# Attention, two expert layers and a gate in one kernel: the counts as a running sum, two groups' attention sums with the queries in the rows, and a longer planned wait for GpSimd

## The chip, the core and the metric

One core of a Trainium2 chip runs the whole program. The metric is device microseconds of one execution; lower is better. The engines are named as the profile names them: PE is TensorE (PEld its weight loads), DVE is VectorE, ACT is ScalarE, POOL is GpSimd, SP is the queue that issues most DMAs.

## What is computed

```
# q, k, v: (2, 8, 768, 64); n_sink = 4; window = 128
keep = (key < n_sink) | ((query - key >= 0) & (query - key < window))
s = where(keep, q @ k.T / sqrt(64), -1e9)
a = exp(s - max(s)); a = a / (sum(a) + 1e-9)
x = (a @ v), heads side by side                 # 1536 tokens x 512
h = x @ w_in; x = max(0.01 * h, h) @ w_out      # 512 -> 2048 -> 512
do = (x @ w_skip) > 0                           # skip gate
e = argmax(x @ w_gate); gate = softmax(x @ w_gate)[e]   # 8 experts
out = x; out[do] += gate * (relu(x @ w1[e]) @ w2[e])    # 512 -> 1024 -> 512
```

All of it is float32.

## The kernel before

The 1536 tokens are six groups g = 0 to 5 of 256 tokens (two tiles of 128 each, twelve tiles t in all). Three stages overlap: attention of a group, the dense layer of a group (sixteen chunks f of 128 hidden columns: `chunk`, L868 for the first product, L889 for the second), and the gate of a group (`gating`). The eight experts come last (`plan_routed`, L1109, L1119, L1126).

**Order.** No engine's order is written by hand. `Plan.op` collects every operation with its engine, a cost in ns, what it reads and writes and a priority; `Plan.run` simulates five queues with these costs, gives each engine the ready operation of lowest priority number for which a buffer is free, and emits instructions in that order. `Plan.gap(a, b)` is the wait that the plan allows between the end of a and the start of a dependent b: 195 ns from PE, 150 ns between other engines. At run time each engine works through its own list strictly in turn. Whether an instruction waits there is decided on the chip, not by the plan.

**Attention of groups 0 and 1** ("whole" in the code) keeps plain float32 matmuls. `blocks` loads q, k and v of the group into buffers of the tag `w`. For v it takes, for every 128 keys, a buffer of 4 x 2 x 128 columns in which each head's 64 columns stand beside 64 columns that POOL has set to zero (L373), so that two heads can add into one 128-row result. For each pair of heads p = 0 to 3, `prep` turns keys and queries (L458, L468; copies on ACT and DVE at L462, L478, L475). For each half qt of the queries, `item` makes for both heads h the scores (PE, L591), adds the mask and takes the row's minimum (DVE, L598), takes the exponential and its sum (ACT, L601), adds 1e-9 and inverts the sums (DVE, L605, L606), scales the weights P by the inverse (L610 on ACT, L613 on POOL), turns P (PE, L629) into a copy AT (ACT, L633), and multiplies (PE, L668) with v as the stationary and AT as the moving operand; keys of the sink block come in by a further matmul per head with `vs` stationary and `wz` (buffer C) moving, for all items but those of group 0. The result PV has the 128 columns of the two heads in its rows and the 128 queries in its columns, which is what the dense layer reads: ACT copies it to x (L674) and DVE makes the low part (L675). The float32 matmuls appear as two records each in the trace.

Group 0 scales head 0 on POOL and head 1 on ACT, group 1 both on ACT, groups 2 to 5 both on POOL.

**Counts.** `gating` needs, for every token of tile t, how many earlier tokens chose the same expert. The one-hot choices of all tiles stand in `oh_all` (128 x 8 for a tile, bfloat16). Tile t takes t matmuls of `ones` against the earlier tiles' one-hots and one of `tri` against its own (L1015), accumulated in PSUM. `count_over` adds up all twelve (L1046). For the last group the two tiles are gated one after the other, and the `ones` part is emitted apart from the `tri` part. There the count is followed by L1024 (DVE, the selection columns `hs`) and L844 (PE, which gathers the first expert's tokens by it). L974 is a small matmul that folds the gate's two half products (`fold`, 18 rows by 9 columns moving).

Of the kernel before, what the change touches and what calls it, by code (L numbers as in the profile page):

```python
# [47 lines left out]
C_TR = 114.0  # L48
C_DMA = 490.0
# [17 lines left out]
class Plan:  # L67
# [166 lines left out]
class Arm:  # L234
# [63 lines left out]
    def keep(self):  # L298

        k = lambda name, shape, dt=F32: self.pool.tile(shape, dt, tag=name, bufs=1, name=name)  # L300
        self.oh_all = k("oh_all", [128, self.NT // 128, self.E], BF16)
        self.rank_all = k("rank_all", [128, self.NT // 128])
        self.gate_all = k("gate_all", [128, self.NT // 128])
        self.nt = k("nt", [128, 2, self.E])
        self.tot = k("tot", [128, 2], I32)
        self.w9 = k("w9", [128, 4, 2, 9], F32R)
        self.ks = k("ks", [128, self.KD, 16])

    def share(self, other):
        for name in ("pool", "psum", "oh_all", "rank_all", "gate_all", "nt", "tot", "w9"):  # L310
            setattr(self, name, getattr(other, name))


# [24 lines left out]
    def blocks(self, g, b, qp):  # L338

        P, nc, io = self.p, self.nc, self.io  # L340
        if qp == 0:
            self.raws = {}
        pr = -60 if g == 0 else -13.5
        def ld(t, a, p0, p1):

            heads, n = slice(2 * p0, 2 * p1), p1 - p0
            src = io[t][b, heads, 128 * a:128 * a + 128, :]
            if t != "v":
                eng, dma = ("ACT", nc.scalar) if g == 0 and t == "k" and p0 == 0 else ("SP", nc.sync)
                x = self.raws[t, a // 2]  # L350
                P.op(eng, C_DMA, lambda: dma.dma_start(
                    out=x.tile[:, a % 2, 128 * p0:128 * p1].rearrange("p (h d) -> p h d", d=64), in_=src.rearrange("h p d -> p h d")),
                    w=[(x, (a % 2, p)) for p in range(p0, p1)], pr=pr, lat=64 * n * 1024 / 200.0)
                return
            x = self.raws[t, a]
            for h in range(2):
                P.op("SP", C_DMA, lambda h=h: nc.sync.dma_start(
                    out=x.tile[:, p0:p1, h, 64 * h:64 * h + 64], in_=io["v"][b, 2 * p0 + h:2 * p1:2, 128 * a:128 * a + 128, :].rearrange("h p d -> p h d")),
                    w=[(x, (h, 0))], pr=pr, lat=32 * n * 1024 / 200.0)

        new = range(2 * qp, 2 * qp + 2)
        for t in "qk":
            self.raws[t, qp] = P.buf("w", [128, 2, 512])
        for p0, p1 in ((0, 1), (1, self.KD)) if g == 0 else ((0, self.KD),):
            for t in "kq":
                for a in new:
                    ld(t, a, p0, p1)
            if p0 == 0:
                for a in new:

                    x = self.raws["v", a] = P.buf("w", [128, self.KD, 2, 128])
                    for h in range(2):
                        P.op("POOL", 100 + 0.9 * 256, lambda x=x, h=h: nc.gpsimd.memset(x.tile[:, :, h, 64 - 64 * h:128 - 64 * h], 0.0), w=[(x, (h, 1))], pr=pr)  # L373
                    if g:
                        ld("v", a, 0, self.KD)
        if g == 0:
            for a in new:
                ld("v", a, 0, self.KD)

    def load(self, g, b, qp, p):  # L380

# [18 lines left out]
    def sinks_v(self, g, b, whole):  # L400
        P, nc, io = self.p, self.nc, self.io
        pr = 16 * (g - 1) - 7
        src = lambda h: io["v"][b, h:self.H:2, 0:16, :].rearrange("h s d -> s h d")
        vs = self.vs = P.buf("vs", [128, self.KD, 2, 128], F32 if whole else F32R)
        if whole:
            def ld():
                for h in range(2):
                    nc.sync.dma_start(out=vs.tile[h:32:2, :, h, 64 * h:64 * h + 64], in_=src(h))
# [4 lines left out]
            P.op("POOL", 1000, lambda: nc.gpsimd.memset(vs.tile, 0.0), w=[vs], pr=pr - 7)  # L413
# [152 lines left out]
    def item(self, g, qp, p, qt, whole):  # L566

        P, nc, c = self.p, self.nc, self.c
        pr = self.order(g, p, qt)
        qb = 2 * qp + qt  # L570
        one, sink = qb == 0, qb >= 2
        ncol = 128 if one else 272
# [11 lines left out]
        sm = P.buf("s4", [128, 2])  # L584
# [19 lines left out]

        P.op("DVE", 70, lambda: nc.vector.tensor_scalar(out=sm.tile, in0=sm.tile, scalar1=1e-9, scalar2=None, op0=ALU.add), w=[sm], pr=pr)  # L605
        P.op("DVE", 81, lambda: nc.vector.reciprocal(out=sm.tile, in_=sm.tile), w=[sm], pr=pr)  # L606
        for h in range(2):
            if g == 1 or g == 0 and h:

                P.op("ACT", c_act(ncol, False), lambda h=h: nc.scalar.activation(out=A.tile[:, 0:ncol, h], in_=A.tile[:, 0:ncol, h], func=AF.Copy, scale=sm.tile[:, h:h + 1]),  # L610
                     r=[sm], w=[(A, h)], pr=pr)
# [25 lines left out]
                out=x.tile[:, :, 1, :], in0=tt.tile[:, 2 * i:2 * i + 2, :], in1=x.tile[:, :, 0, :].bitcast(F32), op=ALU.subtract), r=[tt, (x, 0)], w=[(x, 1)], pr=pr)  # L637
        js = [1] if one else [qt, qt + 1]
        if whole:
            vb = [self.raws["v", 2 * qp - 1 + j] for j in js]  # L640
            rd = [*AT, *vb]
            vblk = lambda i, h: vb[i].tile[:, p, h, :]
        else:
            rd = [*AT, vh]
            vblk = lambda i, h: vh.tile[:, js[i], h, :]
# [12 lines left out]
        vs = self.vs  # L658
        pv = P.buf(spare if g == 2 else "PV", [128, 2, 256])

        def pvmm():
            for h in range(2):
                mm = [(vblk(i, h), at(i, h)) for i in range(len(js))]
                if sink:
                    mm.append((vs.tile[:, p, h, :], wz.tile if whole else self.sAT.rearrange("p a b -> p (a b)")))
                for n, (l, r) in enumerate(mm):
                    to = pv.tile[:, 0, 0:128] if whole else pv.tile[:, h, :]
                    nc.tensor.matmul(out=to, lhsT=l, rhs=r, start=n == 0 and not (whole and h), stop=n == len(mm) - 1 and (h == 1 or not whole))  # L668

        P.op("PE", (nj + 2 * sink) * (213 if whole else c_mm(256)), pvmm, r=rd, w=[pv], pr=pr)  # L670
        if whole:
            xT = self.xt[g]
            x = lambda i: xT.tile[:, i, p, 128 * qt:128 * qt + 128]
            P.op("ACT", c_act(128, True), lambda: nc.scalar.activation(out=x(0), in_=pv.tile[:, 0, 0:128], func=AF.Copy), r=[pv], w=[(xT, (p, 0, qt))], pr=pr)  # L674
            P.op("DVE", c_dve(128), lambda: nc.vector.tensor_tensor(out=x(1), in0=pv.tile[:, 0, 0:128], in1=x(0).bitcast(F32), op=ALU.subtract),  # L675
                 r=[pv, (xT, (p, 0, qt))], w=[(xT, (p, 1, qt))], pr=pr)
            return
        xr = self.xr[g, p]

# [239 lines left out]
    def gating(self, g, acc, own):  # L919
# [89 lines left out]
        for m, x in enumerate(x2):  # L1009
            cp = P.buf(("S", "PV")[own[0]] if last else "T", [128, E])  # L1010

            def count(ts, m=m, cp=cp):
                for t in ts:
                    mine = t == tiles[m]
                    nc.tensor.matmul(out=cp.tile, lhsT=c["tri" if mine else "ones"], rhs=self.oh_all[:, t, :], start=t == 0, stop=mine)  # L1015

            ts = range(tiles[m] + 1)
            for part in ([ts[:-1], ts[-1:]] if last else [ts]):
                counted = P.op("PE", 30 * len(part), lambda part=part, count=count: count(part), r=[("oh", t) for t in part], w=[cp], pr=pr)
            fill(0, counted)  # L1020
            rk = self.rank_all[:, tiles[m]:tiles[m] + 1]
            if last:
# [16 lines left out]
    def count_over(self):  # L1039
# [427 lines left out]
```

## Time and profile before

| | |
|---|---|
| time, median of 3 runs (lowest to highest) | 541.52 us (540.7 to 542.23) |
| the profiled execution's own time | 538.87 us |
| its span, first to last instruction | 537.1 us |
| busy share PE, DVE, ACT, POOL | 96%, 77%, 65%, 31% |
| mean granted TensorE clock | 0.996 of full speed |

The profile is of one execution. Its time is 1.77 us over its span, and 2.65 us under the median of the runs. An engine's busy time counts overlapping records once. A busy PE need not be at its peak, since ends of matmuls are modelled; the time from one matmul's start to the next one's is what it costs in a row of them.

### The profile page before, as it was taken

How to read it: one execution, taken by the hardware profiler on the slowest of the kernel's cores; microseconds unless marked ns; L12 is line 12 of the kernel's file. 1: busy time of each engine (PE TensorE's matmuls, PEld its weight loads, DVE VectorE, ACT ScalarE, POOL GpSimd, SP SyncE). 2: the span in 40 equal slices, each digit the busy share in tenths (PEclk: the TensorE clock that was granted, in tenths of full speed). 3: DMA queues.
4: the chain of work that ended last, by engine and by line, in shares of the span. 5: the costliest groups of instructions: out<-in, count | busy, mean ns of one | idle time of the engine just before them, and what ended most of it. 6: DMA issues, size and time to landing. Idle time of an engine off the chain costs nothing.

```text
span 537.1 us, 10336 instructions
## 1 busy us (share of the span) xinstructions
PE 516.7 (96%) x3353; PEld 452.7 (84%) x3353; DVE 412.5 (77%) x1167; ACT 349.6 (65%) x912; POOL 168.0 (31%) x288
## 2 busy tenths in 40 slices
PE   7889999999999999999999999999999999999994
PEld 4679998988888889998989988999898778888883
DVE  4899999998677787778767876665756587888881
ACT  5898766554576767676667775655566277666760
POOL 5322021331165343333333342220221024455332
PEclk9999999999999999999999999999999999999998
DMA  8999444631111212223112220106476269989750
GB/s 151 292 313 330 162 158 115 189 94 31 59 42 23 70 42 46 49 51 90 31 43 49 50 81 12 25 1 237 135 214 190 94 240 343 290 272 329 263 170 20
DMA packets 83807, 72.46 MB, mean 135 GB/s; under 512 B 56563, under 2 KB 64755, under 8 KB 83744
## 3 DMA queue, kind: packets, MB, share of 16 engines
q1 hardware_dynamic: 81456, 70.54, 43.6%
q0 software_dynamic: 1600, 1.04, 0.6%
q8 instruction: 29, 0.48, 0.4%
q14 instruction: 34, 0.28, 0.2%
q10 hardware_dynamic: 688, 0.13, 0.1%
HBM read 65.40 MB, written 10.51 MB: 141 GB/s over the span
## 4 chain that ended last, share of the span: by engine, by line
PE 80%; DVE 9%; ACT 6%; issue 2%; POOL 1%; DMA 1%; POOLq 0%; DVEq 0%; ACTq 0%
PE h L868 21%; PE acc L889 18%; PE acc L1126 8%; PE PV L668 5%; PE h L1109 4%; PE T L629 3%; PE PV L1109 2%; PE S L1109 2%; PE S L595 2%; PE S L889 2%; PE PV L889 2%; ACT P L601 2%; PE T L1119 1%; DVE C L684 1%; PE S L591 1%
## 5 line engine op out<-in xcount | busy, mean ns | idle before, releaser
L868 PE MATMUL h<-x,w 128*128 128x256 f32 x1128 | 155.1, 287 | 0.8 <-DVE gl L882 0.8
L868 PEld LDWEIGHTS h<-x,w 128*128 128x128 f32 x1128 | 143.6, 190 | 4.9 <-DVE gl L882 1.8
L889 PE MATMUL acc<-w,gh 128*128 128x512 f32 x308 | 100.1, 406 | 0.0
L879 ACT ACTIVATE t<-h 128x256 f32<-128x256 f32 x94 | 35.8, 381 | 40.6 <-PE h L868 40.1
L889 PE MATMUL acc<-w,gl 128*128 128x512 f32 x156 | 61.3, 393 | 0.0
L613 POOL TENSOR_SCALAR P<-P,s 128x272 f32<-128x272 f32 (+1 forms) x72 | 39.9, 566 | 65.6 <-DVE s L606 55.1
L601 ACT ACTIVATE P<-P,s 128x272 f32<-128x272 f32 (+1 forms) x96 | 50.1, 522 | 15.3 <-DVE s L598 14.1
L889 PEld LDWEIGHTS acc<-w,gh 128*128 128x128 f32 x308 | 53.3, 189 | 7.5
L880 DVE TENSOR_TENSOR h<-h,t 128x256 f32<-128x256 f32 x94 | 40.2, 428 | 22.1 <-ACT t L879 21.5
L721 DVE TENSOR_TENSOR w<-wm,w 128x1024 fp32r<-128x1024 f32 x36 | 49.5, 1383 | 5.0 <-ACT w L714 2.8
L881 ACT ACTIVATE gh<-h 128x256 fp32r<-128x256 f32 x92 | 34.8, 379 | 21.0 <-DVE h L880 20.4
L714 ACT ACTIVATE w<-wm 128x1024 fp32r<-128x1024 f32 x44 | 44.9, 1056 | 5.0 <-PE h L868 3.9
L882 DVE TENSOR_TENSOR gl<-h,gh 128x256 fp32r<-128x256 f32 x92 | 38.5, 418 | 10.2 <-ACT gh L881 8.9
L598 DVE CUSTOM_DVE_ANT_0 P<-S,mk 128x272 f32<-128x272 f32 (+1 forms) x70 | 28.9, 413 | 11.2 <-PE S L595 9.9
L714 ACT ACTIVATE w<-wf 128x512 fp32r<-128x512 f32 x52 | 31.7, 625 | 8.3 <-DVE wf L754 6.4
L889 PEld LDWEIGHTS acc<-w,gl 128*128 128x128 f32 x156 | 29.3, 188 | 6.7
L721 POOL TENSOR_TENSOR w<-wm,w 128x1024 fp32r<-128x1024 f32 x8 | 19.9, 2483 | 45.5 <-ACT w L714 21.9
L685 POOL TENSOR_TENSOR xr<-C 128x128 f32<-128x128 f32 x32 | 15.9, 497 | 55.6 <-DVE C L684 49.8
L721 DVE TENSOR_TENSOR w<-wf,w 128x512 fp32r<-128x512 f32 x42 | 29.4, 708 | 0.7 <-ACT w L714 0.7
L629 PE MATMUL T<-idt,P 128*128 128x128 f32 x152 | 26.3, 290 | 0.3
L684 DVE TENSOR_TENSOR C<-PV,C 64x256 f32<-64x256 f32 x48 | 20.3, 422 | 7.6 <-ACT C L683 4.7
L629 PEld LDWEIGHTS T<-idt,P 128*128 128x128 f32 x152 | 22.5, 204 | 3.1 <-POOL P L613 1.3
(277 smaller groups left out, 1116.6 us busy)
## 6 DMA issues: line engine op xcount, KB each, us to landing
wm<-in_moe_w_dram SPq DMA_DIRECT2D x44, 512.0 KB, 4.4
w<-in_moe_w_in_dram SPq DMA_DIRECT2D x14, 512.0 KB, 6.2
w<-in_moe_w_out_dram SPq DMA_DIRECT2D x14, 512.0 KB, 7.2
wf<-in_moe_w_dram SPq DMA_DIRECT2D x20, 256.0 KB, 4.2
vs<-in_moe_w_dram SPq DMA_DIRECT2D x10, 512.0 KB, 4.7
rq<-in_q_dram SPq DMA_DIRECT2D x56, 64.0 KB, 2.3
out_dram<-x SPq DMA_DIRECT2D x12, 256.0 KB, 2.4
rk<-in_k_dram SPq DMA_DIRECT2D x24, 96.0 KB, 2.4
```

The costliest lines, as they stand in the source:

```text
L601: P.op("ACT", 280 + 0.83 * ncol, lambda h=h: nc.scalar.activation(out=A.tile[:, 0:ncol, h], in_=A.tile[:, 0:ncol, h], func=AF.Exp, scale=- ...
L613: P.op("POOL", 245 + 0.83 * ncol, lambda h=h: nc.gpsimd.tensor_scalar(out=A.tile[:, 0:ncol, h], in0=A.tile[:, 0:ncol, h], scalar1=sm.tile[ ...
L629: nc.tensor.transpose(tt.tile[:, 2 * j + h, :], A.tile[:, o:o + 128, h], c["idt"])
L714: nc.scalar.activation(out=at(0), in_=view(src.tile), func=AF.Copy)
L721: P.op(lo, {"DVE": c_dve(n), "POOL": c_pool2(n)}[lo], lambda: eng[lo].tensor_tensor(out=at(1), in0=view(src.tile), in1=at(0).bitcast(F32), ...
L868: nc.tensor.matmul(out=h.tile, lhsT=wi.tile[:, a, 128 * k:128 * k + 128], rhs=xT.tile[:, b, k, :], start=k == 0 and n == 0, stop=k == self ...
L879: P.op("ACT", c_act(256, True), lambda: nc.scalar.activation(out=t.tile, in_=h.tile, func=AF.Copy, scale=0.01), r=[h], w=[t], pr=fast)
L880: P.op("DVE", c_dve(256), lambda: nc.vector.tensor_tensor(out=h.tile, in0=h.tile, in1=t.tile, op=ALU.max), r=[t], w=[h], pr=fast)
L882: P.op("DVE", c_dve(256), lambda: nc.vector.tensor_tensor(out=gl.tile, in0=h.tile, in1=gh.tile.bitcast(F32), op=ALU.subtract), r=[h, gh], ...
L889: nc.tensor.matmul(out=acc[i].tile, lhsT=a.tile[:, q], rhs=wo.tile[:, b, :], start=first and n == 0, stop=last and n == 2)
L1109: nc.tensor.matmul(out=hp[a].tile, lhsT=xt.tile[:, i, k, :], rhs=w1[k][j].tile[:, 512 * a:512 * a + 512], start=k == 0 and n == 0, stop=k ...
L1126: nc.tensor.matmul(out=yp.tile, lhsT=gt.tile[:, a, 2 * n + j, :], rhs=w2[n][b].tile[:, 512 * j:512 * j + 512], start=n == 0 and j == 0 and ...
```

## The change

Three edits. First, `Plan.gap` returns 255 instead of 150 ns from ACT or DVE to POOL. Second, `so_far` (128 x 8, bfloat16) holds the sum of the one-hots of all tiles before the current one: a tile takes one matmul of `ones` against it and one of `tri`, DVE then adds the tile to it, and `count_over` takes one matmul. Third, in groups 0 and 1 the weights P are turned unscaled; AT is the stationary operand and v, 64 columns of one head, the moving one, so that PV has queries in its rows; ACT scales each head's 64 columns by the inverse sum on the way out of PSUM (into y, a buffer of the tag `qT`), PE turns the 128 x 128 result, and ACT and DVE make x from that. The zeroed halves of v go, and with them the memsets; v takes half the space and half as many load instructions.

```diff
@@ Plan.gap
+        if b.eng == "POOL" and a.eng != "PE":
+            return 255.0
         return 195.0 if a.eng == "PE" else 150.0
@@ blocks
-            x = self.raws[t, a]
-            for h in range(2):
-                P.op("SP", C_DMA, lambda h=h: nc.sync.dma_start(
-                    out=x.tile[:, p0:p1, h, 64 * h:64 * h + 64], in_=io["v"][...]...
-                    x = self.raws["v", a] = P.buf("w", [128, self.KD, 2, 128])
-                    for h in range(2):
-                        P.op("POOL", 100 + 0.9 * 256, lambda x=x, h=h: nc.gpsimd.memset(x.tile[:, :, h, 64 - 64 * h:128 - 64 * h], 0.0), ...
-        for t in "qk":
+        for t in "qkv":
             self.raws[t, qp] = P.buf("w", [128, 2, 512])
@@ item
-        for h in range(2):
-            if g == 1 or g == 0 and h:
-
-                P.op("ACT", c_act(ncol, False), lambda h=h: nc.scalar.activation(out=A.tile[:, 0:ncol, h], ..., scale=sm.tile[:, h:h + 1]),
-                     r=[sm], w=[(A, h)], pr=pr)
-                continue
+        for h in [] if whole else range(2):
             P.op("POOL", 245 + 0.83 * ncol, lambda h=h: nc.gpsimd.tensor_scalar(
...
+        def rows():
+
+            mm = [(pv.tile[:, 0, 0:128], wz.tile, vs.tile[:, p, :])] if sink else []
+            mm += [(pv.tile[:, 0, 64 * h:64 * h + 64], at(i, h), vblk(i, h)) for h in range(2) for i in range(len(js))]
+            for n, (to, l, r) in enumerate(mm):
+                nc.tensor.matmul(out=to, lhsT=l, rhs=r, start=n == 0, stop=n == len(mm) - 1)
...
-        P.op("PE", (nj + 2 * sink) * (213 if whole else c_mm(256)), pvmm, r=rd, w=[pv], pr=pr)
+        P.op("PE", (nj + sink) * 222 if whole else (nj + 2 * sink) * c_mm(256), rows if whole else pvmm, r=rd, w=[pv], pr=pr)
...
-            P.op("ACT", c_act(128, True), lambda: nc.scalar.activation(out=x(0), in_=pv.tile[:, 0, 0:128], func=AF.Copy), r=[pv], ...
+            y = P.buf("qT", [128, 128])
+            def scale():
+                for h in range(2):
+                    nc.scalar.activation(out=y.tile[:, 64 * h:64 * h + 64], in_=pv.tile[:, 0, 64 * h:64 * h + 64], func=AF.Copy, scale=sm.tile[:, h:h + 1])
+            P.op("ACT", 2 * c_act(64, True), scale, r=[pv, sm], w=[y], pr=pr)
+            tx = P.buf("T", [128, 128])
+            P.op("PE", C_TR, lambda: nc.tensor.transpose(tx.tile, y.tile, c["idt"]), r=[y], w=[tx], pr=pr)
+            P.op("ACT", c_act(128, True), lambda: nc.scalar.activation(out=x(0), in_=tx.tile, func=AF.Copy), r=[tx], ...
@@ gating
+            def count(parts, t=t, cp=cp):
+                for i in parts:
+                    nc.tensor.matmul(out=cp.tile, lhsT=c["tri" if i else "ones"], rhs=(self.oh_all[:, t, :] if i else self.so_far), start=i == 0 or t == 0, stop=i == 1)
...
+                d(70, lambda t=t: V.tensor_tensor(out=self.so_far, in0=self.so_far, in1=self.oh_all[:, t, :], op=ALU.add), [("oh", t)], ["far"])
@@ count_over
-        P.op("PE", 30 * NTL, lambda: [nc.tensor.matmul(out=cp.tile, lhsT=c["ones"], rhs=self.oh_all[:, t, :], ...) for t in range(NTL)], ...
+        P.op("PE", 40, lambda: nc.tensor.matmul(out=cp.tile, lhsT=c["ones"], rhs=self.so_far, start=True, stop=True), r=["far"], ...
```

Where the instructions stand, at three places. A row names the line, the result, its operands and the shape; a number behind a name tells one buffer from the next, and lines of the changed kernel differ from those before by up to 20.

PE in group 0, from the first item's turning of P (result acc) to the second item's product, before:

```order
L629 MATMUL acc_231<-idt,P_185 128x128 x2
L468 MATMUL T_240<-idt,w_139 128x128 x2
L668 MATMUL PV_249<-AT_232,w_141 128x128 x2
L629 MATMUL acc_258<-idt,P_195 128x128 x4
L591 MATMUL h_268<-kT_208,w_149 128x128
L591 MATMUL h_277<-kT_208,w_149 128x128
L591 MATMUL S_281<-kT_208,w_149 128x272
L668 MATMUL PV_290<-AT_259,w_141 128x128
```

The same place now:

```order
L611 MATMUL acc_211<-idt,P_177 128x128 x2
L611 MATMUL acc_224<-idt,P_185 128x128 x4
L455 MATMUL T_235<-idt,w_140 128x128 x2
L455 MATMUL T_245<-idt,w_140 128x128 x2
L648 MATMUL PV_250<-w_151,AT_212 128x64 x2
L578 MATMUL h_256<-kT_200,w_153 128x128
L578 MATMUL h_266<-kT_200,w_153 128x128
L670 MATMUL T_269<-idt,qT_263 128x128
L648 MATMUL PV_274<-w_151,AT_225 128x64 x4
L578 MATMUL S_291<-kT_200,w_153 128x272
L670 MATMUL T_300<-idt,qT_288 128x128
```

P of the second item is turned directly behind the first, the product has 64 columns per head, and each product is followed, two rows or one row of scores later, by the new turning of its scaled result (L670).

PE in group 1, one item's turning, a chunk's second product and another item's product, before (the last three rows stand a second time for the other head):

```order
L629 MATMUL T_658<-idt,P_556 128x128 x4
L651 MATMUL T_670<-idt,P_556 32x128
L591 MATMUL S_674<-kT_489,w_149 128x272
L889 MATMUL acc_681<-w_431,gh_653 128x512 x2
L889 MATMUL acc_681<-w_431,gl_672 128x512
L668 MATMUL PV_701<-AT_659,w_256 128x128
L668 MATMUL PV_701<-AT_659,w_274 128x128
L668 MATMUL PV_701<-C_137,vs_156 128x128
```

The same place now:

```order
L886 MATMUL acc_675<-w_405,gh_651 128x512 x2
L886 MATMUL acc_675<-w_405,gl_659 128x512
L670 MATMUL T_690<-idt,qT_661 128x128
L648 MATMUL PV_694<-vs_142,C_138 128x128
L648 MATMUL PV_694<-w_253,AT_654 128x64 x4
L578 MATMUL S_709<-kT_504,w_153 128x272
L455 MATMUL T_717<-idt,w_238 128x128 x2
L670 MATMUL T_720<-idt,qT_712 128x128
```

The item's product is five matmuls instead of six, and its result is turned after three more matmuls and, in other items, after a chunk's product.

DVE in the gate of the tile before the last (oh_all is the tile's one-hot, hs the selection columns that L844 waits for, wl the low part that the last tile's gate product waits for), before:

```order
L1006 TENSOR_SCALAR sm_6276<-sm_6276 128x1
L995 CAST hs_5545<-oh_all 128x1
L1002 RECIPROCAL gate_all<-sm_6276 128x1
L1007 SCALAR_TENSOR_TENSOR sm_6276<-sm_6276 128x1
L956 TENSOR_TENSOR wl_6267<-T_6266,wl_6267 128x256
L1004 COPY x_1275_5900<-gate_all 128x1
L1024 TENSOR_SCALAR hs_5545<-hs_5545,S_6189 128x128
```

The same place now:

```order
L1003 TENSOR_SCALAR sm_6268<-sm_6268 128x1
L992 CAST hs_5533<-oh_all 128x1
L999 RECIPROCAL gate_all<-sm_6268 128x1
L1004 SCALAR_TENSOR_TENSOR sm_6268<-sm_6268 128x1
L1019 TENSOR_TENSOR so_far<-so_far,oh_all 128x8
L1001 COPY x_1309_5921<-gate_all 128x1
L1026 TENSOR_SCALAR hs_5533<-hs_5533,S_6190 128x128
L1029 ISA sm_6268,rank_all<-S_6190,oh_all 128x8
L1029 ISA rank_all 128x1
L953 TENSOR_TENSOR wl_6259<-T_6258,wl_6259 128x256
```

The new sum stands ahead of the selection, and the low part of the last tile has moved behind it.

## Rows read from the trace of the kernel before

**Rows 1.** The page's first part: busy time, share, instructions of each engine.

```profile
PE 516.7 (96%) x3353; PEld 452.7 (84%) x3353; DVE 412.5 (77%) x1167; ACT 349.6 (65%) x912; POOL 168.0 (31%) x288
```

**Rows 2.** Windows: length, then each engine's busy us, clock, DMA share, GB/s.

```profile
10.00:40.00 30.00, 25.34 (x166) 20.76 (x167) 24.93 (x90) 27.75 (x91) 9.62 (x22) 1.00 1.05 289
40.00:130.00 90.00, 89.14 (x595) 80.87 (x593) 88.13 (x227) 60.12 (x166) 19.04 (x30) 1.00 0.50 158
130.00:410.00 280.00, 277.45 (x1952) 251.73 (x1951) 200.70 (x678) 183.16 (x532) 90.80 (x187) 1.00 0.26 71
410.00:430.00 20.00, 19.16 (x145) 15.03 (x144) 12.31 (x56) 8.52 (x26) 1.79 (x2) 1.00 0.38 116
```

**Rows 3.** PE's waits from 8 to 45 us: in total, times, longest.

```profile
PE acc L629 <- POOL P L613: 3.0, 4, 1.4
PE PV L668 <- ACT AT L633: 0.9, 2, 0.7
```

**Rows 4.** Timeline of the first items: start, length, engine, instruction, [idle before].

```profile
10.36 0.38 POOL L613 TENSOR_SCALAR P<-P,s 128x128 f32<-128x128 f32 x1 [2.41 <-DVE s L606]
...
10.79 0.59 PE L629 MATMUL acc<-idt,P 128*128 128x128 f32 x2 [0.93 <-POOL P L613]
...
11.57 0.40 ACT L633 ACTIVATE AT<-acc 128x256 f32<-128x256 f32 x1
...
12.03 0.71 PE L668 MATMUL PV<-AT,w 128*128 128x128 f32 x4
...
12.78 0.28 ACT L674 ACTIVATE x<-PV 128x128 fp32r<-128x128 f32 x1
```

**Rows 5.** Timeline of PE, one item's product in group 1 and what follows.

```profile
48.58 0.61 PE L668 MATMUL PV<-AT,w 128*128 128x128 f32 x4
...
49.92 0.62 PE L591 MATMUL S<-kT,w 128*128 128x272 f32 x2
50.38 0.38 PE L458 MATMUL T<-idt,w 128*128 128x128 f32 x2
...
50.84 1.69 PE L868 MATMUL h<-x,w 128*128 128x256 f32 x12
```

**Rows 6.** L974, nine columns moving: duration min/median/max; four in a row.

```profile
L974 PE MATMUL T<-fold,wl x24: 252/252/273, 143.1 to 426.5; 18*128 18x9 f32 x24
...
143.14 0.61 PE L974 MATMUL T<-fold,wl 18*128 18x9 f32 x4
```

**Rows 7.** Timeline of PE, the counts of the last group and `count_over`.

```profile
414.80 0.41 PE L1015 MATMUL S<-oh_all,ones 128*128 128x8 bf16 x10
...
426.00 0.42 PE L1015 MATMUL PV<-oh_all,ones 128*128 128x8 bf16 x11
...
427.89 0.44 PE L1046 MATMUL T<-oh_all,ones 128*128 128x8 bf16 x12
```

**Rows 8.** ACT's groups by shape (busy, mean ns | idle before); a pair.

```profile
L610 ACT ACTIVATE P<-P,s 128x272 f32<-128x272 f32 x20 | 10.1, 542 | 1.1 <-DVE s L606 1.1
...
L674 ACT ACTIVATE x<-PV 128x128 fp32r<-128x128 f32 x16 | 4.3, 268 | 4.5 <-PE PV L668 4.4
...
L610 ACT ACTIVATE P<-P,s 128x128 f32<-128x128 f32 x4 | 1.6, 408 | 0.1
...
35.55 0.99 ACT L610 ACTIVATE P<-P,s 128x272 f32<-128x272 f32 x2
```

**Rows 9.** Timeline of DVE and PE in the gate of the last tiles.

```profile
424.82 0.42 DVE L956 TENSOR_TENSOR wl<-T,wl 128x256 fp32r<-128x256 f32 x1
...
425.22 0.34 DVE L1024 TENSOR_SCALAR hs<-hs,S 128x128 f32<-128x128 f32 x1
...
425.30 0.29 PE L966 MATMUL PV<-wl,w 128*18 128x128 f32 x2 [0.47 <-DVE x L1004]
...
426.35 0.38 PE L974 MATMUL T<-fold,wl 18*128 18x9 f32 x2
...
427.11 0.15 DVE L997 TENSOR_TENSOR sm<-T,sm 128x8 f32<-128x8 f32 x1
```

More of the change, by code (lines that the diff above doesn't have):

```diff
@@ L309, in share @@
     def share(self, other):
-        for name in ("pool", "psum", "oh_all", "rank_all", "gate_all", "nt", "tot", "w9"):
+        for name in ("pool", "psum", "oh_all", "so_far", "rank_all", "gate_all", "nt", "tot", "w9"):
             setattr(self, name, getattr(other, name))
@@ L347, in ld @@
             src = io[t][b, heads, 128 * a:128 * a + 128, :]
[L348 to L354, printed above, removed]
-            x = self.raws[t, a]
-            for h in range(2):
-                P.op("SP", C_DMA, lambda h=h: nc.sync.dma_start(
-                    out=x.tile[:, p0:p1, h, 64 * h:64 * h + 64], in_=io["v"][b, 2 * p0 + h:2 * p1:2, 128 * a:128 * a + 128, :].rearrange("h p d -> p h d")),
-                    w=[(x, (h, 0))], pr=pr, lat=32 * n * 1024 / 200.0)
+            eng, dma = ("ACT", nc.scalar) if g == 0 and t == "k" and p0 == 0 else ("SP", nc.sync)
+            x = self.raws[t, a // 2]
+            P.op(eng, C_DMA, lambda: dma.dma_start(
+                out=x.tile[:, a % 2, 128 * p0:128 * p1].rearrange("p (h d) -> p h d", d=64), in_=src.rearrange("h p d -> p h d")),
+                w=[(x, (a % 2, p)) for p in range(p0, p1)], pr=pr, lat=64 * n * 1024 / 200.0)
         new = range(2 * qp, 2 * qp + 2)
-        for t in "qk":
+        for t in "qkv":
             self.raws[t, qp] = P.buf("w", [128, 2, 512])
@@ L367, in blocks @@
                     ld(t, a, p0, p1)
-            if p0 == 0:
-                for a in new:
-                    x = self.raws["v", a] = P.buf("w", [128, self.KD, 2, 128])
-                    for h in range(2):
[L373 to L378, printed above, removed]
+        for a in new:
+            ld("v", a, 0, self.KD)
     def load(self, g, b, qp, p):
@@ L666, in pvmm @@
                 for n, (l, r) in enumerate(mm):
-                    to = pv.tile[:, 0, 0:128] if whole else pv.tile[:, h, :]
-                    nc.tensor.matmul(out=to, lhsT=l, rhs=r, start=n == 0 and not (whole and h), stop=n == len(mm) - 1 and (h == 1 or not whole))
-        P.op("PE", (nj + 2 * sink) * (213 if whole else c_mm(256)), pvmm, r=rd, w=[pv], pr=pr)
+                    nc.tensor.matmul(out=pv.tile[:, h, :], lhsT=l, rhs=r, start=n == 0, stop=n == len(mm) - 1)
+        P.op("PE", (nj + sink) * 222 if whole else (nj + 2 * sink) * c_mm(256), rows if whole else pvmm, r=rd, w=[pv], pr=pr)
         if whole:
@@ L1010, in gating @@
             cp = P.buf(("S", "PV")[own[0]] if last else "T", [128, E])
[L1012 to L1019, printed above, removed]
+            t = tiles[m]
+            def count(parts, t=t, cp=cp):
+                for i in parts:
+                    nc.tensor.matmul(out=cp.tile, lhsT=c["tri" if i else "ones"], rhs=(self.oh_all[:, t, :] if i else self.so_far), start=i == 0 or t == 0, stop=i == 1)
+            before = ["far"] if t else []
+            for parts in ([(0,), (1,)] if last else [(0, 1) if t else (1,)]):
+                counted = P.op("PE", 40 * len(parts), lambda parts=parts, count=count: count(parts), r=[x for i in parts for x in ([("oh", t)] if i else before)], w=[cp], pr=pr)
+            if t:
+                d(70, lambda t=t: V.tensor_tensor(out=self.so_far, in0=self.so_far, in1=self.oh_all[:, t, :], op=ALU.add), [("oh", t)], ["far"])
+            else:
+                d(70, lambda: V.tensor_copy(self.so_far, self.oh_all[:, 0, :]), [("oh", 0)], ["far"])
             fill(0, counted)
@@ L1045, in count_over @@
         cp = P.buf("T", [128, E])
-        P.op("PE", 30 * NTL, lambda: [nc.tensor.matmul(out=cp.tile, lhsT=c["ones"], rhs=self.oh_all[:, t, :], start=t == 0, stop=t == NTL - 1)
-                                      for t in range(NTL)], r=[("oh", t) for t in range(NTL)], w=[cp], pr=pr)
+        P.op("PE", 40, lambda: nc.tensor.matmul(out=cp.tile, lhsT=c["ones"], rhs=self.so_far, start=True, stop=True), r=["far"], w=[cp], pr=pr)
         n = P.buf("sm", [128, E], I32)
```

20 lines of the change are left out of this document (10 added, 10 removed).

## The prediction

> **What bounds the kernel now.** I read the page's busy shares first: PE is busy 96% of the span, no other engine over 77% [rows 1]. So an edit counts by the PE work that it adds or takes, except where PE waits. The windows say where that is [rows 2]. From 130 to 410 us PE idles 2.55 of 280 us, from 40 to 130 us 0.86 of 90, although DVE is nearly as full there (88.13). From 10 to 40 us, attention of group 0, PE idles 4.66 of 30 us and ACT is the fullest engine, 27.75. From 410 to 430 us, the gate of the last tiles, PE idles 0.84. The list of PE's waits gives the cause in group 0: 3.0 us in four waits for POOL to scale P, 0.9 us for ACT's copies [rows 3]. The clock is at its upper level, 2.4 GHz, in all four stretches (1.00 in [rows 2]), so it is no term here.
>
> **Group 1's product on PE.** An item of group 1 takes six matmuls of two records each. One item's twelve records run from 48.58 to 49.92, where scores follow: 1.34 us, 112 ns from start to start [rows 5]. The first four end after 0.61, so a single record lasts 0.61 - 3 x 0.112 = 0.27 us. Now an item takes five matmuls and one turning. What a record costs with 64 moving columns no row shows; the nearest is L974, with the same 128 stationary columns and only nine moving ones: (0.61 - 0.252)/3 = 119 ns from start to start [rows 6]. So fewer moving columns save nothing, and I take 112. The turning is one record of 0.38 - 0.27 = 0.11 us, by the pair of turnings at 50.38 [rows 5]. An item then takes 10 x 0.112 + 0.11 = 1.23 us for 1.34; eight items save 0.9 us, in a stretch where PE is full.
>
> The Trainium skill, TensorE: Matmul & The Clock Gate, section "Back-to-back issue gap", has the gap of an isolated matmul grow with its moving columns (N/2.4 + 2.5 ns), by which half the columns would cost about half. Its section "LDWEIGHTS" has the load grow with the stationary columns, and L974 speaks for the second. By the first the change would gain some 3.5 us more; that case is priced below from rows.
>
> **Counts on PE.** A count matmul costs (0.41 - 0.17)/9, (0.42 - 0.17)/10, (0.44 - 0.17)/11, each 25 ns [rows 7]. Tile t had t + 1 and now has 2 (tile 0 keeps 1). Tiles 2 to 9 save 1 to 8, that is 36, and 36 x 25 = 0.9 us in a full PE. Tile 10 saves 9 of the ten at 414.80, 0.2 us. Tile 11 saves 10 and `count_over` 11, but both lie in the gate of the last tiles, where PE waits for DVE anyway: 0, at most 0.5 us.
>
> **Group 0.** It gains the waits for POOL, up to 3.0 us. Against that stand three prices. Eight turnings add 0.9 us to PE; about half of it falls into idle time, so 0.45. ACT loses eight scalings of P (four of 128, four of 272 columns) and gets sixteen of 64 columns from PSUM. One of 64 columns lies between 211 ns (from 268 at 128 columns, L674, down by the 0.9 ns a column between L610's 408 and 542) and 348 (from L610's 408, the same way) [rows 8]; a pair overlaps by 0.09 (0.99 for two of 542), so it takes 0.33 to 0.61 us. I take 0.55, as L610 too reads its scale from a tile. Eight pairs are 4.4 us for 4 x 0.408 + 4 x 0.542 = 3.8: ACT, the fullest engine, gets 0.6 us more (from -1.2 to +1.1).
>
> The third price is a new wait. After the product's last record PE must wait for its end (0.27 - 0.11 = 0.16), ACT's start (0.04, from 12.74 to 12.78), the pair (0.55) and the way back (0.06, from 11.97 to 12.03) [rows 4, 5]: 0.8 us, and what stands in PE's list between product and turning must fill it. Scores of 272 columns take 0.46 (49.92 to 50.38), and of 128 columns half of that, by 112 ns a record. Of the eight items of group 0 four have only 0.36 to 0.46 us between, as in the first piece shown of the new list (two scores of 128, then one of 272). They are short by 0.35 us each, 1.4 in all. Behind the waiting turning stand the next scores and products. 3.0 - 0.45 - 0.6 - 1.4 leaves a gain of 0.5 us. It can reach 3.0 if the new waits fall where PE idles anyway, and turn into a loss of 1.5 if ACT takes its 1.1 more and the waits only change their name.
>
> **The same wait in group 1** is covered: six of the eight items have a chunk's product between (twelve matmuls take 1.69 to their end, at 50.84 [rows 5]), one has 1.1 us of scores and turnings, and one 0.68, as in the second piece: 0.1 us lost. ACT loses 16 scalings there (eight pairs of 0.99) and gets eight pairs of 0.55. It has idle time from 40 to 130 us [rows 2], so that gives nothing.
>
> **The gate of the last tiles.** DVE has one addition more before the selection, by the nearest row (427.11) at most 0.15 us; and the low part of the last tile (424.82) now stands behind the selection (425.22), so that the last tile's gate product comes some 0.5 us later than 425.30, the length of the selection and what follows it, while the gather of the tile before comes sooner [rows 9]. L974 waited behind eleven counts until 426.35; those are gone, so it moves little. I take a loss of 0.2 us (from -0.2 to +0.6). The other additions, 12 x 0.15 us on DVE, lie where DVE is busy 72% (200.70 of 280); without that cover they would cost 1.8 us.
>
> **At nothing.** The memsets and POOL's scaling in group 0 leave POOL, which idles 20 of 30 us there. Half of v's load instructions go, but the bytes are the same and the DMA share is 1.05, so loads land no sooner; if they did, DVE would still be the one to decode the weights. The longer gap to POOL changes no instruction, only the order: the pieces of attention and dense work in groups 2 to 5 change places. What that can win is bounded by PE's idle 2.55 us from 130 to 410, and it can lose as much; I take 0.
>
> **Sum.** -0.5 (group 0) - 0.9 (product) + 0.1 - 0.9 - 0.2 (counts) + 0.2 (gate) = -2.2 us. From the execution's own 538.87 (span 537.1 and 1.77 around it) this makes 536.7. The median of the runs is 2.65 higher, 541.52, and from there it is 539.3. That is 0.4%; a change under 0.3% (1.6 us) can hardly be told from none here.
>
> **The rivals.**
>
> *ACT holds group 0.* ACT's 27.75 of 30 us and the added pairs take back what POOL gives up: group 0 loses the 1.1 us of the upper bound instead of winning 0.5. For it: after POOL's, the waits are for ACT. Against: ACT idles 2.25 us there, in part because P comes late. -2.2 + 1.6 = -0.6 us, 540.9: no change. 17 in 100.
>
> *All of POOL's wait comes back.* The new turnings wait only where PE would have idled, and P's two buffers come free sooner. Group 0 gains 3.0: -2.2 - 2.5 = -4.7, 536.8. For it: ACT and PE both have idle time there. Against: PE's list runs strictly in turn. 15 in 100.
>
> *Slower: the turnings hold PE.* If ACT is busy with another operation when a product ends (it is busy 60.12 of 90 us there, and an operation on 272 columns takes 0.54), each of the sixteen turnings waits 0.35 us like the four of group 0: twelve more, 4.2 us. -2.2 + 4.2 = +2.0, 543.5. It decides for slower by over 1.6 us from 0.32 us on at each of the twelve. For it: the plan prices the pair at 0.21 us where rows give 0.55. Against: the cover in group 1. The order of groups 2 to 5 could add to it, but not alone. 13 in 100.
>
> *The moving columns set the price after all.* A record of 64 columns costs 56 ns: 32 matmuls of group 1 save 64 x 0.056 = 3.6 us more, 535.7. Against it is L974; for it, only that L974 fills 18 rows. 5 in 100. This is what the gap rule of the Trainium skill's TensorE: Matmul & The Clock Gate, named above, would make of it.
>
> **How the numbers follow.** The sum holds in 50 of 100; three quarters of that are beyond 0.3%. Faster: 0.38 + 0.15 + 0.05 = 0.58. Same: 0.12 + 0.15 of ACT's case = 0.27. Slower: 0.13 and the rest of ACT's, 0.15. The range goes from 536.2, with all of POOL's wait and some of the order's bound, to 542.8, with the order's bound lost and half of the turnings' waits.
>
> **What would show it.** Right: PE's waits for POOL are gone before 40 us, waits of about 0.35 us for ACT stand before some turnings of group 0 and hardly any in group 1; records of 64 columns start 112 ns apart; a tile's counts take two matmuls; the whole pattern of dense chunks after 40 us stands about 0.5 us earlier. Wrong: turnings that wait in group 1; records 56 ns apart; idle PE from 130 to 410 us well off 2.55; a gate of the last tiles longer by more than 0.6 us.

## The result: slower by 0.6%

The changed kernel takes 543.97 us (median of 6 runs, 542.28 to 544.05) against 541.11 us before (6 runs); the ratio is 1.0061, 95% interval 1.0041 to 1.0082, that is 2.2 to 4.4 us more. The prediction was 2.2 us less. The profiled execution has a span of 542.2 us.

First what answers to the rows of before. The page's first part and the windows of the changed kernel, columns as in [rows 1, 2]:

```profile
PE 519.7 (96%) x3287; PEld 452.0 (83%) x3287; DVE 411.5 (76%) x1179; ACT 347.0 (64%) x920; POOL 159.8 (29%) x272
```

```profile
10.00:40.00 30.00, 26.71 (x180) 21.66 (x178) 25.26 (x92) 27.59 (x98) 4.14 (x10) 1.00 1.01 297
40.00:130.00 90.00, 89.64 (x597) 80.89 (x597) 88.21 (x230) 59.24 (x169) 17.36 (x32) 1.00 0.49 155
130.00:410.00 280.00, 274.35 (x1875) 247.11 (x1874) 200.21 (x682) 179.53 (x526) 89.17 (x185) 0.99 0.25 68
410.00:430.00 20.00, 19.24 (x119) 15.30 (x117) 11.72 (x38) 9.63 (x25) 2.56 (x2) 1.00 0.45 153
```

Before 130 us it goes as hoped: PE idles 3.29 us from 10 to 40 us instead of 4.66. The loss is in the third row: 5.65 us of idle PE instead of 2.55, and a mean clock of 0.99. PE's waits from 8 to 45 us, for [rows 3]; no line for POOL is left:

```profile
PE PV L648 <- ACT AT L615: 0.8, 2, 0.5
PE T L670 <- ACT kT L449: 0.5, 1, 0.5
...
PE T L670 <- ACT qT L666: 0.2, 1, 0.2
```

The timeline of PE for one item of group 1, for [rows 5], and ACT's scaling by shape, for [rows 8]:

```profile
48.20 0.38 PE L648 MATMUL PV<-vs,C 128*128 128x128 f32 x2
48.42 1.00 PE L648 MATMUL PV<-w,AT 128*128 128x64 f32 x8
49.26 0.68 PE L578 MATMUL S<-kT,w 128*128 128x272 f32 x2
...
51.20 0.27 PE L670 MATMUL T<-idt,qT 128*128 128x128 f32 x1
51.31 0.62 PE L578 MATMUL S<-kT,w 128*128 128x272 f32 x2
```

```profile
L666 ACT ACTIVATE qT<-PV,s 128x64 f32<-128x64 f32 x32 | 8.2, 309 | 1.5 <-PE PV L648 1.3
```

Eight records of 64 columns take 0.84 us from start to start, 105 ns each, and the turning 0.11 without a wait.

**Where the time goes.** The timeline of PE and SP, between the end of group 2's attention and the start of group 3's:

```profile
169.99 1.16 SPq L936 DMA_DIRECT2D out_dram<-x  x2
...
170.69 0.64 PE L611 MATMUL T<-idt,P 128*128 128x128 f32 x4
172.80 0.44 PE L491 MATMUL T<-idt,rk 128*128 128x128 f32 x2 [1.47 <-DMA out_dram<-x]
173.72 0.44 PE L691 MATMUL T<-idt,rq 128*128 128x128 f32 x2 [0.47 <-ACT rk L495]
173.91 0.48 PE L656 MATMUL acc<-AT,vhl 128*128 128x256 f32 x2
...
176.00 1.12 PE L949 MATMUL T<-idt,x 128*128 128x128 f32 x4 [0.47 <-DVE qT L694]
176.77 0.67 PE L582 MATMUL S<-kT,qT 128*128 128x128 f32 x2
177.95 0.61 PE L963 MATMUL T<-wl,w 128*18 128x128 f32 x4 [0.52 <-DVE wl L953]
```

The same stretch before, group 1's result leaving and the last product of group 2's attention:

```profile
171.06 0.40 PE L668 MATMUL acc<-AT,vhl 128*128 128x256 f32 x2
...
174.36 1.55 SPq L939 DMA_DIRECT2D out_dram<-x  x2
```

Before, group 2's last product (171.06) came ahead of the end of group 1's dense layer (174.36), and its chunks filled PE in between. Now the dense layer has ended at 169.99 and the last product comes at 173.91. Chunks of group 2 can't start until that attention is through: PE starts no chunk's product from 169.63 to 180.96, and what it waits for there (1.47, 0.47, 0.47, 0.52 and 0.23 us) is work of ACT and DVE. (The profile names a DMA at 172.80. The weight load of that turning, at the same time, waits for DVE's sAT, L637, and so does the turning in run 9, so I take it to be DVE.) Then the clock falls. Windows of PE: length, busy, granted clock, DMA share, GB/s:

```profile
170.00:174.00 4.00, 2.06 (x17) 1.00 0.37 137
174.00:178.00 4.00, 3.01 (x19) 0.62 0.16 37
178.00:182.00 4.00, 3.77 (x26) 0.53 0.17 39
182.00:186.00 4.00, 4.00 (x28) 1.00 0.26 59
```

PE was busy 2.06 of 4 us, and then stood at 1.2 GHz for about 6.8 us, until shortly before 182. I call this stretch the handover. In the table below its measure is PE's busy time from 165 to 190 us.

### The profile page after: what moved, and what is told of

Its sections match the earlier page's. It is cut to its first block, busy times and chain, and to the rows that moved or that the text cites. A ratio compares the mean times of both kernels' runs of the same rounds, so it can differ in the third digit from the quotient of the medians.

```text
span 542.2 us, 10201 instructions
## 1 busy us (share of the span) xinstructions
PE 519.7 (96%) x3287; PEld 452.0 (83%) x3287; DVE 411.5 (76%) x1179; ACT 347.0 (64%) x920; POOL 159.8 (29%) x272
## 5 line engine op out<-in xcount | busy, mean ns | idle before, releaser
L595 POOL TENSOR_SCALAR P<-P,s 128x272 f32<-128x272 f32 (+1 forms) x64 | 32.3, 518 | 32.0 <-DVE s L593 21.9
L611 PE MATMUL T<-idt,P 128*128 128x128 f32 x152 | 27.5, 292 | 0.7 <-POOL P L595 0.4
L617 ACT ACTIVATE AT<-T 128x256 fp32r<-128x256 f32 x60 | 20.3, 382 | 11.0 <-PE T L611 10.3
```

The source lines that it names most:

```text
L611: nc.tensor.transpose(tt.tile[:, 2 * j + h, :], A.tile[:, o:o + 128, h], c["idt"])
```

## The experiments

Each was timed beside the kernel before. "Rows" is the third edit, "sum" the second, "gap" the first.

| run | edits | ratio to before (95%) | PE busy of 25 us, clock |
|---|---|---|---|
| before | none | | 23.89, 1.00 |
| changed | rows, sum, gap | 1.0061 (1.0041 to 1.0082) | 21.79, 0.86 |
| 1 | rows, sum | 1.0028 (1.0014 to 1.0041) | 21.58, 1.00 |
| 2 | gap | 1.0169 (1.0146 to 1.0193) | 22.10, 0.93 |
| 3 | rows, gap | 1.0065 (1.0046 to 1.0084) | 21.75, 0.93 |
| 4 | sum, gap | 1.0157 (1.0134 to 1.0181) | 22.10, 0.93 |
| 5 | all, constant 9 | 1.0031 (1.0018 to 1.0044) | 23.34, 1.00 |
| 6 | rows, sum, constant 9 | 0.9970 (0.9957 to 0.9983) | 23.34, 1.00 |
| 7 | constant 9 alone | 1.0006 (0.9988 to 1.0024) | 24.21, 1.00 |
| 8 | sum | 1.0026 (1.0015 to 1.0038) | 23.55, 1.00 |
| 9 | all, PE filled | 1.0067 (1.0051 to 1.0084) | 22.61, 1.00 |
| 10 | sum, old costs | 1.0044 (1.0022 to 1.0066) | 23.78, 1.00 |
| 11 | rows, constant 9 | 0.9969 (0.9957 to 0.9982) | 23.62, 1.00 |
| 12 | rows, sum, constant 9, old costs | 0.9977 (0.9962 to 0.9992) | 23.64, 1.00 |
| 13 | as 12, additions late | 0.9970 (0.9955 to 0.9985) | 23.64, 1.00 |
| 14 | rows | 1.0042 (1.0026 to 1.0058) | 21.59, 0.93 |

**Runs 1 to 4: which edit.** In run 1 the gap is taken back:

```diff
-        if b.eng == "POOL" and a.eng != "PE":
-            return 255.0
```

> The changed kernel with the old gap to POOL (150 ns); the running sum and the queries in the rows stay. Theory A (the lost time comes from the new order at the handover from group 1 to group 2, 171 to 182 us, where PE has 32 rows in a row without a dense chunk; the plan makes that stretch only when the gap and the rows edit come together): PE is full from 170 to 180 us, idle PE from 130 to 410 us is back near 2.5 us, no low clock there, and the time is 1.5 to 3 us under the kernel before (ratio 0.994 to 0.998). Theory B (the turnings and ACT's scaling cost more than estimated): still 1 to 3 us over the kernel before (ratio 1.002 to 1.006).

Slower by 0.28%. The handover stands empty without the gap too (21.58 of 25 us), so "only when the gap and the rows edit come together" was wrong. Run 2 has the gap alone:

> The kernel before with only the longer gap to POOL (255 ns). Theory A: no stretch without dense work at the handover from group 1 to group 2, within 2.5 us of the kernel before (ratio 0.996 to 1.004). Theory C (the longer gap by itself spoils the order of groups 2 to 5): 3 to 5 us over the kernel before (ratio 1.006 to 1.009), with idle PE and a low clock somewhere between 130 and 410 us.

The worst of all, and theory C (1.006 to 1.009) named too little. PE's waits from 8 to 45 us:

```profile
PE acc L631 <- POOL P L615: 6.4, 4, 2.3
```

That is 6.4 us for POOL where [rows 3] had 3.0. The gap moves POOL's scalings in group 0, too, and empties the handover (22.10). In the changed kernel POOL scales nothing in groups 0 and 1, so this first part doesn't fall on it.

> Queries in the rows and the longer gap, the counts as before. Theory A: the same stretch at 171 to 182 us as in the changed kernel, with a low clock behind it, and the counts' matmuls on top: 0.5 to 1.5 us over the changed kernel (ratio to before 1.007 to 1.011). Theory B, too: over before. If the running sum is what made the stretch: at or under the kernel before.

> Running sum and the longer gap, groups 0 and 1 as before. Theory A: no such stretch; the counts' saving of about 1 us and the order's share: ratio 0.995 to 1.002. Theory C: over the kernel before by 2 us or more (ratio over 1.004).

Run 3 is the changed kernel without the sum, and as slow; run 4 is run 2 with the sum, and hardly faster. The 0.9 us of the counts don't show in either pair.

**Runs 5 to 7: the handover filled.** Group 2's items get another place among the priorities, nothing else changes:

```diff
-        return 16 * (g - 1) + 4 * p + 2 * qt - (21 if g < 2 else 10 if g == 2 else 5)
+        return 16 * (g - 1) + 4 * p + 2 * qt - (21 if g < 2 else 9 if g == 2 else 5)
```

> The changed kernel with one constant of the plan's priorities different: group 2's items stand 9 instead of 10 behind in `order`. All three edits stay. In PE's list the dense chunks of group 1 are then spread up to the handover to group 2, and no 32 rows in a row without one are left. Theory A (the loss is the unfilled handover and the low clock behind it, not the edits' own work): PE full and the clock at 1.00 from 165 to 185 us, 4 to 6 us under the changed kernel, ratio to the kernel before 0.993 to 0.998. Theory B (the edits' own work costs more than estimated): still over the kernel before.

> As the run before, but with the old gap to POOL (150 ns). Theory A, if the gap acts only through the order: within 1.5 us of that run. If the longer gap costs or gains by itself, beyond that.

> Control: the kernel before with the same constant (9 instead of 10) and none of the three edits. Theory A: its handover had work already, so the constant gives little, ratio 0.997 to 1.003. If the constant by itself is the gain, the ratio is that of the two runs above.

With one number changed, PE is busy 23.34 us in the handover at full clock, and the order without the gap goes from 1.0028 (run 1) to 0.9970 (run 6), 3.1 us, with intervals far apart. The constant alone gives nothing (run 7). So the work of rows and sum is no loss, their order is: theory B falls. But run 5 gains only 1.6 us on the changed kernel where 4 to 6 were expected, and lies 3.3 us over run 6, its twin without the gap. Their handovers are alike; from 185 to 410 us PE idles 3.99 us in run 5 (1.98 up to 300, 2.01 behind) and 2.37 in run 6. The gap's order costs there again. The longest entry in the list of PE's waits of run 5 from 185 to 418 us is this one, and run 6's list has no such entry:

```profile
PE T L633 <- DVE qT L694: 1.8, 4, 0.6
```

That is the turning of P's 32 sink rows, held up four times behind DVE's work on qT. Of the 2.7 us between the two spans (539.8 and 537.1) the idle time is 1.6, and 0.5 stands there at the first turning of P already (10.13 and 9.61).

**Run 9: the clock.** Ten matmuls that compute nothing stand in PE's list where it idled:

```diff
         P.op("PE", nj * C_TR, tr, r=[A], w=[tt], pr=pr, hold=AT)
+        if (g, p, qt) == (2, 3, 1):
+            self.filler(6, pr)
...
```

(Six of the ten; the other four stand likewise at two more places.)

> The changed kernel, every engine's order kept, with ten matmuls added to PE's list that compute nothing used (ones into a free bank of h): six behind the last turning of P in group 2, two behind the turning of keys that follows, two in the gate of group 1, that is, where PE stands idle from 171 to 176 us. Theory clock (of the loss at the handover, about 2.6 us is the low clock that follows the idle PE, the rest the waits themselves): the clock stays at 1.00 from 175 to 182 us, the useful work waits as before, and the time is 2 to 3 us under the changed kernel (ratio to the kernel before about 1.001). Theory waits only: the clock is no cause, the time stays (ratio 1.006).

The windows of the handover, columns as above:

```profile
170.00:174.00 4.00, 3.78 (x25) 1.00 0.38 138
174.00:178.00 4.00, 2.63 (x20) 1.00 0.16 37
178.00:182.00 4.00, 3.24 (x34) 1.00 0.22 50
```

The clock stays up, and the time stays too (1.0067). At 2.4 GHz PE waits more from 174 to 182 us (2.13 us idle instead of 1.22): there the chain through ACT and DVE ends last, not PE. The first fifteen matmuls of group 2's chunks are through 1.0 us earlier (they start at 180.37 and take 2.01 us, for 180.96 and 2.38 in the changed kernel), and the span is 541.4 for 542.2. The 2 to 3 us that I had put down to the clock are refuted; a gain of up to 1 us is not, by these intervals.

**Runs 11 and 14: rows alone.** One constant apart, 9 and 10:

> Queries in the rows alone, with the constant 9 for group 2; no running sum, no longer gap. Theory A: group 0 and 1 give 2 to 2.5 us and nothing takes them back at the handover: ratio 0.995 to 0.997. It also says what the running sum gives on top of this in the run with both (0.997): by its terms 0.9 us, by the trace of that run a loss of about 0.5.

> Queries in the rows alone, with the constant of before (10), no running sum and no longer gap. If the order at the handover is lost through the rows edit itself: PE idle 2 to 4 us between 165 and 190 us, ratio 1.000 to 1.003, where the same work with the constant 9 gave 0.9969. If it needs the running sum beside it: ratio 0.995 to 0.998.

0.9969 and 1.0042: the same edit wins 1.7 us or loses 2.3, by its order. Rows alone, with the constant of before, empty the handover; it needs neither sum nor gap. The executions of run 14 also differ among themselves: three of the twelve had a mean clock of 0.996 and took 540.41 to 540.51 us, nine had 0.993 (the profiled one among them, with its low clock behind the handover) and took 541.94 to 543.31. Even the three are over the median of the kernel before beside them, 539.36, and run 11 is under its. Whether the clock makes the 2 us between the two kinds, or goes along with longer waits, no run here shows. In run 11 the order from group 2 on is nearly that of before, so that one row can be held against its twin. The turning of the queries of group 2's last pair and POOL's first long operation for the experts, run 11 and then before:

```profile
148.35 0.38 PE L523 MATMUL T<-idt,rq 128*128 128x128 f32 x2
...
383.33 2.42 POOL L715 TENSOR_TENSOR w<-wm,w 128x1024 fp32r<-128x1024 f32 x1 [19.88 <-ACT sm L993]
```

```profile
150.29 0.38 PE L539 MATMUL T<-idt,rq 128*128 128x128 f32 x2
...
384.86 2.42 POOL L721 TENSOR_TENSOR w<-wm,w 128x1024 fp32r<-128x1024 f32 x1 [19.85 <-ACT sm L999]
```

Up to that turning 1.94 us are gained, and 1.53 of them are left at 383 us. Part of this is how an execution starts: runs 12 and 13, with nearly the same order up to there, have the turning at 148.91 and 148.57, and their first turning of P starts at 9.95 and 9.63 instead of 9.45. So groups 0 and 1 give 1.4 to 1.9 us. In the changed kernel the queries' turning for that pair stands ten us behind the turning of its keys:

```profile
148.22 0.49 PE L520 MATMUL T<-idt,rk 128*128 128x128 f32 x3
...
158.20 0.38 PE L526 MATMUL T<-idt,rq 128*128 128x128 f32 x2
```

That row alone doesn't empty the handover: in run 7 it stands as late (157.31), and PE is busy 24.21 us there.

**Runs 8, 10, 12 and 13: the running sum.**

> The kernel before with the running sum alone. The prediction's terms for it: 0.9 and 0.2 us less for the counts, 0.2 more in the gate of the last tiles: 0.9 us faster, ratio 0.998. Theory A: the turning of the queries of group 2's last pair stands behind 18 dense matmuls in this order too, so idle PE at 165 to 185 us may eat it: ratio up to 1.002.

1.0026, a loss of 1.4 us, and the order differs again. Runs 10 and 12 give the plan the costs of before for the counts and 0 for the additions, so that the order nearly stays; each addition goes behind the selection:

```diff
-                d(70, lambda t=t: V.tensor_tensor(out=self.so_far, ...
+                late(0, lambda t=t: V.tensor_tensor(out=self.so_far, ...
```

> The kernel before with the running sum alone, but the plan is given the costs of before for the counts and nothing for the additions, and each addition has a priority number higher by 0.1, so that it stands behind the selection; nearly the whole order of before is kept. Theory A (the running sum saves what was estimated, and its loss in the run of the sum alone came with the order): 0.9 to 1.3 us faster than before, ratio 0.9975 to 0.9985. If the additions themselves cost on DVE: 1.000 or over.

> Queries in the rows and the running sum with the constant 9, without the longer gap; counts and additions have the plan's costs of the kernel before, as in the run of the sum in the old order. Theory A: both savings hold, 3 to 3.5 us faster than before, ratio 0.9935 to 0.9955, and 1 us under the rows alone. If the additions cost on DVE: not under the rows alone.

Run 10 is no gain, and its executions spread from 539.37 to 545.05 us, in step with the mean granted clock: 0.997 in the shortest, 0.994 or 0.995 up to 540.8, 0.991 to 0.994 from there to 544.5, 0.989 in the two longest. Which of the two brings the other about is not shown. Run 12 is not under run 11. Between these two a place can be named. The timeline of run 12 near 383 us, POOL, DVE and PE:

```profile
383.36 2.38 POOL L716 TENSOR_TENSOR w<-wm,w 128x1024 fp32r<-128x1024 f32 x1 [19.89 <-PE T L1012]
...
383.46 2.30 DVE L1018 TENSOR_TENSOR so_far<-so_far,oh_all 128x8 bf16<-128x8 bf16 x1
...
385.75 0.40 DVE L875 TENSOR_TENSOR h<-h,t 128x256 f32<-128x256 f32 x1
...
385.81 0.18 PE L1012 MATMUL T<-so_far,ones 128*128 128x8 bf16 x1 [1.04 <-DVE so_far L1018]
```

and of run 11, the same place without the sum:

```profile
383.70 0.43 DVE L874 TENSOR_TENSOR h<-h,t 128x256 f32<-128x256 f32 x1
...
384.35 1.42 DVE L1025 SCALAR_TENSOR_TENSOR sm<-rank_all,sm 128x1 int32<-128x1 f32 x1
```

An addition of 8 columns lasts 2.30 us: it ends at 385.76, with POOL's operation (385.74). The next tile's count waits for it, and so does the chunk's maximum (385.75 instead of 383.70). Run 13 lets the second tile count the first one's choices by a matmul of its own and puts both additions behind both counts:

```diff
+            if pair:
+                sets = [(2, 1) if t == 1 else (0, 2, 1)]
...
```

> As the run of rows and sum with old costs (0.9977), but the second tile of a group counts the first tile's one-hots by a matmul of its own, so that no count waits for the addition of the same group, and both additions stand behind both counts. One count matmul more for five tiles. Theory port (an addition with both inputs in SBUF is held as long as POOL's operation runs, and the count and the maximum behind it with it): PE's wait of 1.2 us near 385 us goes, about 0.9 us under that run, ratio 0.9955 to 0.9965. Theory count (two counts cost no less than many): no change, 0.9975 to 0.998.

PE has no wait left from 380 to 390 us. The addition is still held, for 1.45 us, but PE doesn't wait for it:

```profile
383.54 0.43 DVE L875 TENSOR_TENSOR h<-h,t 128x256 f32<-128x256 f32 x1
...
384.14 1.45 DVE L1023 TENSOR_TENSOR so_far<-so_far,oh_all 128x8 bf16<-128x8 bf16 x1
```

The ratio moves from 0.9977 to 0.9970, where 0.9955 to 0.9965 was expected, and less than the intervals can tell. The wait's cause is shown by the traces; its price isn't by the times. Runs 6, 11, 12 and 13 are the versions that beat both kernels, by 0.2 to 0.3% over before.

In the changed kernel no addition is held, but a neighbour is. Its additions, and the same place beside POOL's operation:

```profile
L1019 DVE TENSOR_TENSOR so_far<-so_far,oh_all x11: 136/161/164, 147.2 to 432.3; 128x8 bf16<-128x8 bf16 x11
...
388.71 2.40 POOL L718 TENSOR_TENSOR w<-wm,w 128x1024 fp32r<-128x1024 f32 x1 [22.71 <-PE T L1013]
...
388.81 2.33 DVE L997 TENSOR_SCALAR sm<-sm 128x2 f32<-128x2 f32 x1
```

Here the sum has put a small operation of the gate (L997) where POOL holds DVE, ahead of the chunk's maximum (391.25), and PE waits 0.44 us for what comes of that. Runs 1, 5, 6 and 8 have the same row (2.32 or 2.33 us) and the same 0.44. Before, the held operation (1.42 us) stands behind the maximum, and PE has no wait there.

## Why the prediction was wrong

**The step that failed** is "The longer gap to POOL changes no instruction, only the order ... What that can win is bounded by PE's idle 2.55 us from 130 to 410, and it can lose as much; I take 0." Three things in it don't hold. The gap isn't the only edit that changes the order: rows alone do (run 14), and so does the sum (run 8). The gap's order is not one of groups 2 to 5 only (run 2, group 0). And idle time of before bounds what can be won, but not what can be lost: a new order can make any amount of idle, and the handover alone went from 1.11 us in 25 to 3.21, at a lower clock besides. "The order of groups 2 to 5 could add to it, but not alone" fails with it. One of the prediction's own signs of being wrong did come: from 130 to 410 us PE idles 5.65 us instead of 2.55. The working even had the changed order at hand, and looked at the places of the edits instead of the places where PE's list runs out of chunks.

By the ratios: rows in a good order -1.7 us (run 11), the sum on top +0.4 (run 12, which can't be told from none), back to the constant and costs of the change itself +2.8 (run 1), the gap +1.8 (changed kernel). Together 3.3. Each part is uncertain by 0.7 to 1.3, and its order goes with every step.

**The rivals.** Slower came out with the size of "the turnings hold PE" (543.5), but not by it: no turning waits in group 1, 0.2 us of waits for qT stand in group 0. That the time fell outside the stated range is in part a slip in the sum: "the order's bound lost and half of the turnings' waits" is 2.55 + 2.1 over 539.3, that is 543.95, where the text has 542.8. ACT did not take back what POOL gave up in group 0, as its rival had it: PE idles 1.37 us less there. But 2.3 of the 2.8 us in the list of PE's waits from 8 to 45 us are now for ACT, and so POOL's 3.0 did not all come back either. The moving columns do not set the price: 105 ns against an estimated 112 and a rival's 56. The Trainium skill, TensorE: Matmul & The Clock Gate, section "LDWEIGHTS", has the load of the stationary operand grow with that operand's columns, which are 128 in both kernels. The trace agrees in that half the moving columns take only 7 ns off the 112.

**Groups 0 and 1** were right in kind and near in size: 0.5 + 0.9 - 0.1 = 1.3 us were forecast, 1.4 to 1.9 are read from runs 11 to 13. In run 11 PE idles 3.19 us from 10 to 40 us, for 4.66. The pair on ACT costs 0.52 (0.55 estimated); the third price was too high, 0.7 us of waits before turnings, 0.5 of them for kT, instead of 1.4.

**Counts.** The matmul price held: in run 11 six counts take from 332.97 to 333.13, in run 12 one takes from 333.55 to 333.59. In the changed kernel the additions themselves stay short (164 ns at most), as the prediction had it; PE waits 0.22 us for the last of them, at `count_over`. What was not seen is that they move what POOL holds up (0.44 us above). In runs 10 and 12 an addition itself is held, and there the cover "DVE is busy 72%" fails: it says nothing of which operation stands ahead of which when POOL holds one of them.

**The gate of the last tiles** was right up to the experts. The timeline of the changed kernel:

```profile
428.71 0.18 PE L1013 MATMUL S<-oh_all,tri 128*128 128x8 bf16 x1
...
429.54 0.42 DVE L953 TENSOR_TENSOR wl<-T,wl 128x256 fp32r<-128x256 f32 x1
...
430.02 0.30 PE L963 MATMUL PV<-wl,w 128*18 128x128 f32 x2
...
433.73 0.73 PE L1110 MATMUL S<-w,wl 128*128 128x512 f32 x2
434.34 0.28 DVE L1141 TENSOR_TENSOR wl<-h,wl 128x128 fp32r<-128x128 f32 x1
```

From the tri count to the first expert's product it takes 5.02 us, against 4.78 before (424.64 to 429.42): +0.24, with +0.2 forecast, by the low part (429.54) behind the selection, as the order showed. Not seen was what follows: the first expert's low part (434.34) comes 0.61 us behind the product's start, where before it came with it (429.43), and PE waits 0.21 us for one of these parts.

**Open** is why the plan's order with the gap makes the turnings of run 5 wait for qT, where run 8 loses its 1.4 us beyond the 0.44, and why the clock falls in some executions of runs 10 and 14 and not in others.

## What to carry to other kernels

Where a scheduler sets the order, an edit's price on its own and the price of the new order are two terms, and the second can be the larger: here 4.6 us against 1.3 won. Read the whole new list for the bound engine's filler: stretches without independent work, above all where one stage hands over to the next, are where waits turn up. To learn what an edit is worth, hold the order fixed, or compare several orders.

An engine that is 72% busy is no cover for a small operation on a path (runs 10 and 12). What counts is the operation that may be held there, and who stands behind it.

## What the runs showed of the hardware

A DVE operation can be held as long as a POOL operation runs. The additions of run 12, duration in ns (least, median, most):

```profile
L1018 DVE TENSOR_TENSOR so_far<-so_far,oh_all x11: 146/156/2297, 146.3 to 426.8; 128x8 bf16<-128x8 bf16 x11
```

In run 11 the maximum (0.43 us, one input in PSUM) ran unhindered beside the same POOL operation that held the SCALAR_TENSOR_TENSOR for 1.42. The Trainium skill, SBUF — State Buffer, section "SBUF: two separate sides", says that DVE and GpSimd share one pair of ports as an exclusive lock, for a DVE operation with two inputs in SBUF (against a GpSimd operation that reads SBUF) or in a two-port mode, and that the loser waits for the whole instruction. The trace agrees: the addition's two inputs are in SBUF, and it ends within 0.02 us of POOL's.

In the changed kernel the clock fell to 1.2 GHz behind 4 us in which PE was busy 2.06, for about 6.8 us. Filling them kept it at 2.4 GHz, and the time did not change beyond the intervals (1.0067 for 1.0061): where the other engines' chain sets the end, as there, a low clock of PE cost little. That this holds elsewhere is not shown; in run 14 the executions with the higher mean clock are the shorter ones, by 2 us.
